# An S5 state-space layer and a SwiGLU block in one kernel: token tile 0 loaded in two halves, and the last w_down rows of two more chunks contracted in 32-row pieces

## The chip, the cores and the metric

The kernel runs on one core of one Trainium2 chip. The metric is device microseconds of that core for one execution. Its engines work in parallel and are ordered by semaphores alone: TensorE (PE; matmuls, with its weight loads shown apart as PEld), VectorE (DVE), ScalarE (ACT), GpSimd (POOL) and SyncE (SP). SyncE, ScalarE and GpSimd each have a queue from which they issue DMA transfers; "SPq" and "ACTq" in the profile are such issues. All transfers of the core run on the same 16 DMA engines.

## The reference

Input x has 2048 tokens of 512 values. They are normalized and go through two branches that are added to x:

```python
xn = _layernorm(x, axis=-1)
return x + _A_ref(xn, ...) + _B_ref(xn, B_w_gate, B_w_up, B_w_down)

def _B_ref(x, w_gate, w_up, w_down):          # F = 1376 hidden columns
    g = _silu(x @ w_gate)
    u = x @ w_up
    return (g * u) @ w_down

def _A_ref(x, ...):                           # P = 512 complex states
    Bu = jnp.einsum("bld,pd->blp", x + 0j, B_bar)
    for t in range(L):
        h = Lam_bar[None, :] * h + Bu[:, t, :]
    y = 2.0 * jnp.einsum("blp,dp->bld", hseq, Cmat).real + x * Dskip[None, None, :]
```

Inputs and output are bf16; sums are kept in f32 in PSUM.

## The kernel before

The 2048 tokens are 16 tiles of 128 (on the partitions), in 4 chunks of 4 tiles. For each chunk c there are four pieces of work on TensorE: gate and up projections (`gateup_chunk`, 10 full tiles of 128 hidden columns and a last one of 96; L446, and L501 for the last), the B projection of the state-space branch (`bproj_chunk`, L371), the down projection (`out_ffn`, L587, or in `out_pair`, L559) and the C projection of the states (`out_ssm`, L606). The two output projections of a tile add into one PSUM bank. VectorE does the layer norms, the products g*u, the rotations and the scans over time; ScalarE moves results out of PSUM (L460 with SiLU, L461, L373, L619); GpSimd issues the small copies and the stores that add onto the output, where SyncE has put x before.

The order is written out by hand, and every engine works in that order. Around it stands a small planner: `queue` puts VectorE work into a backlog with an estimated cost, `pump(us)` issues as much of it as TensorE has been given work for, `need(tag)` issues all of a kind before it is used, and `multiply` issues the products g*u that are waiting. The whole goes: a head that treats tiles 0 to 3 one by one, the rest of chunk 0's gate and up, B projections and gate/up of chunk 1, B projection of chunk 2, output of chunk 0 (`out_chunk(0)`), gate/up of chunk 2, B projection of chunk 3, output of chunk 1, gate/up of chunk 3, and the output of chunks 2 and 3 together (`out_pair`).

PSUM has 8 banks of 128x512 f32. `bank()` takes one; it comes free when its last reader is done.

The last 96 hidden columns are the concern of one part of the change. Their product g*u lies in `gu_last`, one of three buffers, with the hidden column on the partition. `product_last` forms it in place (L477). There are two ways to contract it with the last 96 rows of w_down:
- `out_last` (L594): one matmul of the full 128 partitions for each token tile, with zeros in the partitions from 96 on. Chunk 1 has it at the end of `out_ffn`; chunk 0, whose product is not ready then, in `out_end`, after the first gate/up tile of chunk 2, where its four banks are also evicted and stored (`out_leave`, L619 and L620).
- `out_rows` (L547): the 96 rows are cut into three steps of 32, and the four token tiles of a chunk are put side by side on the four groups of 32 partitions, so that four matmuls of 32 partitions each, into four banks, stand behind one another. For this `move_rows` (L186) copies the product into `gu_rows` with 12 small DMAs of GpSimd's queue, and `load_rows` (L180) loads the w_down rows four times over into the place of a B matrix that is no longer read after chunk 3's B projection. Chunks 2 and 3 have this, in `out_pair`.

In the head, SyncE's queue loads, one after the other: x tile 0 (L121), the first gate and up weights (L112), x tiles 2 and 3, the weights of hidden tile 2 (gate, then up), more weights, x tiles 4 to 7 in two transfers (L137), and the B matrices by transposing transfers (L140). ScalarE's queue loads x tile 1, whose memset (L122) makes it wait for VectorE. VectorE takes the statistics of tile 0 in one instruction (L202), those of tile 1 in two halves (L703, L705) with tile 0's normalization (L219) between them. TensorE transposes each tile (L236) and multiplies what there is with the first weights (L695); dummy matmuls (L672) fill the time before.

Of the kernel before, what the change touches and what calls it, by code (L numbers as in the profile page):

```python
# [10 lines left out]
F32 = mybir.dt.float32  # L11
BF16 = mybir.dt.bfloat16
ALU = mybir.AluOpType
ACT = mybir.ActivationFunctionType
# [9 lines left out]
def kernel(  # L24
# [17 lines left out]
    nc = tc.nc  # L42
    _, L, D = A_x.shape
# [3 lines left out]
    CW = 512  # L47
    HW = CW // 2
    NT = L // 128
    NCH = L // CW  # L50
    TPC = CW // 128
    KD = D // 128
    NQ = Pst // 128
    FT = (F + 127) // 128
# [4 lines left out]
    LA, LB = 32, 64  # L59
# [4 lines left out]
    const = ctx.enter_context(tc.tile_pool(name="const", bufs=1))  # L64
# [3 lines left out]
    opool = ctx.enter_context(tc.tile_pool(name="opool", bufs=6))  # L68
# [4 lines left out]
    def bank(shape=(128, CW), dtype=F32):  # L73
        return psum.tile(list(shape), dtype, name="ps")
# [4 lines left out]
    x_v = A_x[0].rearrange("(n p) d -> p n d", p=128)  # L79
# [5 lines left out]
    xall = const.tile([128, NT, D], BF16, name="xall")  # L85
# [10 lines left out]
    wd_sb = const.tile([128, FT, D], BF16, name="wd_sb")  # L96
# [13 lines left out]
    def load_w1(q, tiles, view, gi):  # L110
        a, b = fgroups[gi]
        q.dma_start(out=tiles[gi][:], in_=view[:, :, a * 128:min(F, b * 128)])  # L112
# [5 lines left out]
    nc.scalar.preload_act_table_set("abs_reciprocal_sqrt_and_small")  # L118


    nc.sync.dma_start(out=xall[:, 0, :], in_=x_v[:, 0, :])  # L121
    nc.vector.memset(xall[:, 1, 0:D // 2], 0.0)  # L122
    nc.scalar.dma_start(out=xall[:, 1, :], in_=x_v[:, 1, :])
    load_w1(nc.sync, wg_g, wg_v, 0)
    load_w1(nc.sync, wu_g, wu_v, 0)
# [7 lines left out]
        nc.gpsimd.dma_start(out=prm_rows[i * NQ:(i + 1) * NQ, :], in_=v.rearrange("(q j) -> q j", j=128))  # L133
    load_w1(nc.sync, wg_g, wg_v, 2)
    load_w1(nc.sync, wu_g, wu_v, 2)
    for n in (TPC, TPC + 2):
        nc.sync.dma_start(out=xall[:, n:n + 2, :], in_=x_v[:, n:n + 2, :])  # L137
    for part, src in enumerate((A_B_re, A_B_im)):
        for k in range(KD):
            nc.sync.dma_start_transpose(out=BT[:, part, k, :], in_=src[:, k * 128:(k + 1) * 128])  # L140
# [24 lines left out]

    gu_last = [const.tile([128, CW], BF16, name=f"gu_last{i}") for i in range(3)]
    for t in (*(g[LB + LA:128, :] for g in gu_last), wd_sb[LB + LA:128, FT - 1, :]):
        nc.vector.memset(t, 0.0)  # L170


    RT = 32
    part_end = const.tile([128, D // 2], F32, name="part_end")
    gu_rows = [const.tile([128, 3, 128], BF16, name=f"gu_rows{i}") for i in range(2)]
    wd_rows = BT[:, 0, 0:3, :]

    def load_rows():
        for i in range(TPC):
            nc.gpsimd.dma_start(out=wd_rows[i * RT:(i + 1) * RT], in_=B_w_down[FL:F, :].rearrange("(p f) d -> f p d", f=RT))  # L180

    def move_rows(c):

        for i in range(TPC):
            for p in range(3):
                nc.gpsimd.dma_start(out=gu_rows[c % 2][i * RT:(i + 1) * RT, p, :],  # L186
                                    in_=gu_last[c % 3][p * RT:(p + 1) * RT, i * 128:(i + 1) * 128])

    stats = const.tile([128, NT, 6], F32, name="stats")
    stats_1 = const.tile([128, 2, 6], F32, name="stats_1")  # L190
    mv = const.tile([128, NT, 2], F32, name="mv")
    ve = const.tile([128, NT], F32, name="ve")
# [8 lines left out]
    def ln_stats(n):  # L201
        nc.vector.bn_stats(out=stats[:, n, :], in_=xall[:, n, :])  # L202
        nc.vector.bn_aggr(out=mv[:, n, :], in_=stats[:, n, :])

    def rstd_act(n):

        nc.scalar.activation(out=rstd[:, n:n + 1], in_=mv[:, n, 1:2], func=ACT.Abs_reciprocal_sqrt, bias=EPS)
# [55 lines left out]
    V = nc.vector  # L263
# [205 lines left out]
    def ul(c):  # L469
        if c not in up_last:  # L470
            up_last[c] = up_p.tile([128, CW], BF16, name="ul", bufs=4)
        return up_last[c]

    def product_last(c):
        g, u = gu_last[c % 3][0:LB + LA, :], ul(c)[0:LB + LA, :]
        def mul():
            V.tensor_tensor(out=g, in0=g, in1=u, op=ALU.mult)  # L477
            if c > 1:
                move_rows(c)
        products.append(mul)  # L480

    def up_halves():

        pss = []
        for c in range(0, NCH, 2):
            ps = bank()
            pss.append(ps)
            for k in range(KD):
                for i in range(2):
                    nc.tensor.matmul(ps[i * LB:(i + 1) * LB], lhsT=wu_last[:, k, :],  # L490
                                     rhs=xnT[:, k, (c + i) * CW:(c + i + 1) * CW], start=(k == 0), stop=(k == KD - 1))
        for c in range(NCH):
            i = c % 2
            nc.scalar.copy(out=ul(c)[0:LB, :], in_=pss[c // 2][i * LB:(i + 1) * LB])
        product_last(0)
        product_last(1)

    def gateup_last(c):
        ps = bank()
        for k in range(KD):  # L500
            nc.tensor.matmul(ps[:], lhsT=w_last[:, k, :], rhs=xnT[:, k, c * CW:(c + 1) * CW],  # L501
                             start=(k == 0), stop=(k == KD - 1))
        u = ul(c)
        nc.scalar.activation(out=gu_last[c % 3][0:LB + LA, :], in_=ps[0:LB + LA], func=ACT.Silu)
        nc.scalar.copy(out=u[LB:LB + LA, :], in_=ps[LB + LA:128])
        if c > 1:
            product_last(c)

    def gateup_tile(c, fi):
        if fi == FT - 1:  # L510
            return gateup_last(c)
        psg = bank()
        gu_mm(psg, wg_g, c, fi, 0, CW)
        psu = bank()
        gu_mm(psu, wu_g, c, fi, 0, CW)
        gu_out(c, fi, psg, psu)
# [16 lines left out]
    o_tiles = {}  # L533

    def out_blocks(n):

        return ((0, D // 2), (D // 2, D - 128), (D - 128, D)) if n == NT - 1 else ((0, D),)

    def col_parts(n):
        return ((D // 2, D), (0, D // 2)) if n == NT - 1 else ((0, D),)  # L540

    def out_rows(c, step):

        for i in range(TPC):
            n, rows = c * TPC + i, slice(i * RT, (i + 1) * RT)
            lo, hi = col_parts(n)[-1]
            nc.tensor.matmul(o_tiles[n][0][:, lo:hi], lhsT=gu_rows[c % 2][rows, step, :],  # L547
                             rhs=wd_rows[rows, step, lo:hi], start=False, stop=False)

    def out_pair(c):  # L550

# [28 lines left out]
    def out_ffn(n):  # L580
        c, i = divmod(n, TPC)
        o_tiles[n] = []
        for lo, hi in out_blocks(n):
            o = bank((128, hi - lo))
            o_tiles[n].append(o)
            for fi in range(FT - 1):
                nc.tensor.matmul(o[:], lhsT=gu_tiles[c][:, fi, i * 128:(i + 1) * 128], rhs=wd_sb[:, fi, lo:hi],  # L587
                                 start=(fi == 0), stop=False)
            if c > 0:
                out_last(n, o, lo, hi, False)  # L590

    def out_last(n, o, lo, hi, stop):
        c, i = divmod(n, TPC)
        nc.tensor.matmul(o[:], lhsT=gu_last[c % 3][:, i * 128:(i + 1) * 128], rhs=wd_sb[:, FT - 1, lo:hi],  # L594
                         start=False, stop=stop)

    def out_ssm(n):
# [20 lines left out]
    def out_leave(n, o, res):  # L618
        nc.scalar.copy(out=res[:], in_=o[:])  # L619
        nc.gpsimd.dma_start(out=out_v[:, n, :], in_=res[:], accum_op=ALU.add)  # L620
# [14 lines left out]
    def step():  # L635
        for item in backlog[0:AHEAD + 1]:
            if item[2] is not None:
                item[2]()
                item[2] = None
        cost, op, _, _ = backlog.pop(0)  # L640
        op()
        owed[0] -= cost

    def pump(us):

        owed[0] += us
        while backlog and owed[0] >= backlog[0][0] * 0.5:
            step()
        if not backlog:
            owed[0] = 0.0  # L650

    def multiply(keep):

        while len(products) > keep:
            products.pop(0)()
            owed[0] -= 0.65

    def need(tag):

        while any(item[3] == tag for item in backlog):  # L660
            step()
# [8 lines left out]
    def dummy(n, cols):  # L670
        for _ in range(n):
            nc.tensor.matmul(warm[:, 0:cols], lhsT=ones[:, 0:128], rhs=ones[:, 0:cols], start=True, stop=True)  # L672
# [25 lines left out]
    allk = range(KD)  # L698
    dummy(8, CW)
    dummy(2, 128)  # L700
    ln_stats(0)
    rstd_act(0)
    nc.vector.bn_stats(out=stats_1[:, 0, :], in_=xall[:, 1, 0:D // 2])  # L703
    norm_dve(0)
# [55 lines left out]
    def gateup_chunk(c):  # L760
        for fi in [FT - 1, *range(FT - 1)]:
            gateup_tile(c, fi)
            pump(GU)
            multiply(1)
            if c == 2 and fi == 0:
                out_end(0)

    def out_chunk(c):

        multiply(0)  # L770
        for n in range(c * TPC, (c + 1) * TPC):
            out_ffn(n)
            pump(FT * 0.2163)
        if c == 0:
            need("ln3")
            up_halves()
            multiply(0)
        need(f"ssm{c}")
        need("cf")
        for n in range(c * TPC, (c + 1) * TPC):  # L780
            out_ssm(n)
            pump(2 * NQ * 0.2163)

    def out_end(c):

        for n in range(c * TPC, (c + 1) * TPC):
            o = o_tiles[n][0]
            out_last(n, o, 0, D, True)
            out_leave(n, o, opool.tile([128, D], BF16, name="res"))

    def spread(ops, others, tag, tags):

# [56 lines left out]
    queue_ssm(3)  # L849
    out_chunk(1)  # L850
    gateup_chunk(3)
    out_pair(2)

# [29 lines left out]
```

## Time and profile before

| what | us |
|---|---|
| median of 3 runs | 178.83 (178.77 to 179.09) |
| the profiled execution | 179.21 |
| its span, first to last instruction | 177.4 |
| TensorE busy | 173.1 |
| VectorE busy | 154.6 |
| ScalarE busy | 93.8 |
| GpSimd busy | 39.6 |
| DMA, mean over the span | 91 GB/s |

The granted TensorE clock is full in the whole span. The span is counted from the first instruction; the 1.8 us between it and the execution's time lie around it. Times in the chain, the timeline and the windows are us from the span's start. In the timeline a line is: start, duration, engine, line of the kernel, operation, what it writes <- what it reads, shape, count, and in brackets how long the engine had been idle and what ended that. Instructions of one kind that follow each other are merged. Matmuls overlap: one of 128x512 lasts 0.379 in the record, but the next starts 0.216 after it, so the chain, which counts from start to start, gives the cost.

### The profile page before, as it was taken

Reading aid. Unit: us, or ns where it says so; the run is one execution under the profiler, and the core shown is the slowest. Engines: PE = TensorE matmul, PEld = TensorE weight load, DVE = VectorE, ACT = ScalarE, POOL = GpSimd, SP = SyncE. Lnnn points to the kernel's source line nnn. Section 1 sums busy time; section 2 is a strip of 40 time slices with the busy share of each in tenths; the row PEclk is TensorE's granted clock in tenths of the full one; section 3 lists DMA queues with packets and bytes.
Section 4 is the critical chain, followed back from the end, with each engine's and each line's share of the span. In section 5 each row is a group of like instructions: output and inputs, shape, how many; then the busy total and the mean of one; then the engine's idle time right before and its main releaser. Section 6 shows DMA issues by size and latency. Waiting matters only on the chain.

```text
span 177.4 us, 2510 instructions
## 1 busy us (share of the span) xinstructions
PE 173.1 (98%) x922; PEld 83.1 (47%) x922; DVE 154.6 (87%) x238; ACT 93.8 (53%) x167; POOL 39.6 (22%) x61
## 2 busy tenths in 40 slices
PE   7899999999999999999999999999999999999993
PEld 2784444444444444444444444444444444464443
DVE  6879997999999996899999999999999999991033
ACT  3558898967299649924966662013866610001300
POOL 6050300000300050000709340005186330001410
PEclk9999999999999999999999999999999999999999
DMA  5999857994141015900450011005569600000652
GB/s 172 277 260 202 177 98 142 345 222 105 28 88 34 0 30 118 355 0 0 46 76 15 9 49 43 0 0 59 59 87 181 105 9 0 0 0 4 65 98 76
DMA packets 30092, 16.13 MB, mean 91 GB/s; under 512 B 19296, under 2 KB 29888, under 8 KB 30048
## 3 DMA queue, kind: packets, MB, share of 16 engines
q1 hardware_dynamic: 24800, 11.54, 28.9%
q0 software_dynamic: 4416, 3.87, 15.7%
q10 hardware_dynamic: 864, 0.56, 1.0%
q8 instruction: 7, 0.11, 0.3%
q14 instruction: 5, 0.04, 0.1%
HBM read 8.42 MB, written 5.24 MB: 77 GB/s over the span
## 4 chain that ended last, share of the span: by engine, by line
PE 94%; DMA 3%; SPq 2%; issue 0%; DVE 0%
PE ps L446 36%; PE ps L606 16%; PE ps L371 16%; PE ps L559 10%; PE ps L587 10%; DMA wu<-in_B_w_up_dram 3%; PE ps L501 2%; PE ps L695 2%; PE ps L490 1%; PE ps L594 1%; PE ps L547 1%; SPq L112 1%; SPq L126 0%; SPq L127 0%; SPq L121 0%
## 5 line engine op out<-in xcount | busy, mean ns | idle before, releaser
L446 PE MATMUL ps<-xnT,wg 128*128 128x512 bf16 x148 | 38.0, 379 | 0.0
L446 PE MATMUL ps<-xnT,wu 128*128 128x512 bf16 x148 | 38.0, 379 | 0.0
L413 DVE TENSOR_TENSOR_SCAN g<-r_t,car,u 128x512 bf16<-128x512 f32 x24 | 28.7, 1262 | 0.0
L460 ACT ACTIVATE guT<-ps 128x512 bf16<-128x512 f32 x40 | 24.4, 611 | 7.3 <-PE ps L446 5.2
L371 PE MATMUL ps<-xnT,BT 128*128 128x512 bf16 x128 | 28.3, 379 | 0.0
L606 PE MATMUL ps<-CF,wt 128*128 128x512 bf16 (+2 forms) x144 | 28.2, 355 | 0.0
L461 ACT CAST u<-ps 128x512 bf16<-128x512 f32 x40 | 23.9, 599 | 5.4 <-PE ps L446 5.3
L619 ACT CAST res<-ps 128x512 bf16<-128x512 f32 x12 | 6.8, 594 | 37.5 <-PE ps L606 37.5
L620 POOL DMA_DIRECT2D out_dram<-res x12 | 10.5, 1044 | 59.3 <-ACT res L619 59.3
L446 PEld LDWEIGHTS <-wu 128*128 128x128 bf16 x148 | 14.5, 98 | 17.5
L446 PEld LDWEIGHTS <-wg 128*128 128x128 bf16 x148 | 14.4, 98 | 17.2
L373 ACT CAST u<-ps 128x512 bf16<-128x512 f32 x32 | 18.4, 590 | 5.1 <-PE ps L371 4.9
L606 PEld LDWEIGHTS <-wt 128*128 128x128 bf16 x144 | 13.3, 98 | 14.8 <-issue 0.4
L371 PEld LDWEIGHTS <-BT 128*128 128x128 bf16 x128 | 12.5, 98 | 15.1
L587 PE MATMUL ps<-wd_sb,guT 128*128 128x512 bf16 x80 | 18.1, 379 | 0.0
L559 PE MATMUL ps<-wd_sb,guT 128*128 128x512 bf16 (+1 forms) x90 | 17.6, 355 | 0.0
L211 POOL TENSOR_TENSOR rstd<-ve,neg_half 128x4 f32<-128x4 f32 x3 | 5.2, 1728 | 47.5 <-DVE ve L210 47.5
L186 POOL DMA_DIRECT2D gu_rows<-gu_last x24 | 11.9, 505 | 9.2 <-DVE gu_last L477 6.6
L465 DVE TENSOR_TENSOR guT<-guT,u 128x1024 bf16<-128x1024 bf16 x20 | 13.5, 681 | 0.0
L559 PEld LDWEIGHTS <-guT 128*128 128x128 bf16 x90 | 8.8, 98 | 8.7
L587 PEld LDWEIGHTS <-guT 128*128 128x128 bf16 x80 | 7.8, 98 | 9.4
L611 DVE TENSOR_TENSOR res<-ps,xn_end 128x512 bf16<-128x512 f32 (+1 forms) x4 | 2.5, 626 | 10.6 <-PE ps L606 10.6
(116 smaller groups left out, 196.6 us busy)
## 6 DMA issues: line engine op xcount, KB each, us to landing
out_dram<-in_A_x_dram SPq DMA_DIRECT2D x1, 1536.0 KB, 7.0
out_dram<-res POOLq DMA_DIRECT2D x12, 128.0 KB, 3.2
out_dram<-xall POOLq DMA_DIRECT2D x3, 512.0 KB, 8.2
wd_sb<-in_B_w_down_dram SPq DMA_DIRECT2D x1, 1280.0 KB, 10.2
xall<-in_A_x_dram SPq DMA_DIRECT2D x1, 1024.0 KB, 7.0
wg<-in_B_w_gate_dram SPq DMA_DIRECT2D x1, 512.0 KB, 6.0
wu<-in_B_w_up_dram SPq DMA_DIRECT2D x1, 512.0 KB, 6.9
xall<-in_A_x_dram SPq DMA_DIRECT2D x2, 256.0 KB, 7.1
```

The lines of the kernel that those rows point to most:

```text
L186: nc.gpsimd.dma_start(out=gu_rows[c % 2][i * RT:(i + 1) * RT, p, :], in_=gu_last[c % 3][p * RT:(p + 1) * RT, i * 128:(i + 1) * 128])
L371: nc.tensor.matmul(ps[:], lhsT=BT[:, part, k, q * 128:(q + 1) * 128], rhs=xnT[:, k, c * CW:(c + 1) * CW], start=(k == 0), stop=(k == KD - 1))
L373: nc.scalar.copy(out=u_tiles[c][:, part, q, :], in_=ps[:])
L413: V.tensor_tensor_scan(out=g()[:, part, q, :], data0=r_t[:, q:q + 1].to_broadcast([128, CW]), data1=u_tiles[c][:, part, q, :], initial=ini ...
L446: nc.tensor.matmul(ps[:fs, lo:hi], lhsT=wslice(groups, fi, k), rhs=xnT[:, k, c * CW + lo:c * CW + hi], start=(k == 0), stop=(k == KD - 1))
L460: nc.scalar.activation(out=guT[:fs, fi, :], in_=psg[:fs], func=ACT.Silu)
L461: nc.scalar.copy(out=u_pair[c][:fs, fi % 2, :], in_=psu[:fs])
L465: products.append(lambda: V.tensor_tensor(out=g, in0=g, in1=u, op=ALU.mult))
L559: nc.tensor.matmul(o[:, lo:hi], lhsT=gu_tiles[k][:, fi, i * 128:(i + 1) * 128], rhs=wd_sb[:, fi, lo:hi], start=(fi == 0), stop=False)
L587: nc.tensor.matmul(o[:], lhsT=gu_tiles[c][:, fi, i * 128:(i + 1) * 128], rhs=wd_sb[:, fi, lo:hi], start=(fi == 0), stop=False)
L606: nc.tensor.matmul(o, lhsT=w_tiles[c][:, part, q, i * 128:(i + 1) * 128], rhs=CF[:, part, q, lo:hi], start=(fresh and part == 0 and q == 0 ...
L620: nc.gpsimd.dma_start(out=out_v[:, n, :], in_=res[:], accum_op=ALU.add)
```

## The change

x tile 0 is loaded as two halves of 256 columns, the first on SyncE's queue and the second on ScalarE's, ahead of tile 1, whose memset is gone. Its statistics are taken by halves too, and joined by the aggregation. x tiles 4 to 7 come in one transfer instead of two.

The last 96 hidden columns of chunks 0 and 1 are contracted by `out_rows` as well. Their product is written into the up half's buffer (`ul`) instead of onto the gate's, and `move_rows` copies it from there; `gu_last` has two buffers instead of three, `gu_rows` one for each chunk instead of two in all. `out_ffn` loses its last matmul and `out_end` is gone: chunk 0's four tiles stay in their PSUM banks until, in `out_chunk(1)` behind the down projection of chunk 1, the 24 row pieces of chunks 0 and 1 run, step by step and chunk by chunk, and chunk 0 is evicted and stored.

```diff
-    nc.sync.dma_start(out=xall[:, 0, :], in_=x_v[:, 0, :])
-    nc.vector.memset(xall[:, 1, 0:D // 2], 0.0)
+    nc.sync.dma_start(out=xall[:, 0, 0:D // 2], in_=x_v[:, 0, 0:D // 2])
+    nc.scalar.dma_start(out=xall[:, 0, D // 2:D], in_=x_v[:, 0, D // 2:D])
     nc.scalar.dma_start(out=xall[:, 1, :], in_=x_v[:, 1, :])
...
-    for n in (TPC, TPC + 2):
-        nc.sync.dma_start(out=xall[:, n:n + 2, :], in_=x_v[:, n:n + 2, :])
+    nc.sync.dma_start(out=xall[:, TPC:2 * TPC, :], in_=x_v[:, TPC:2 * TPC, :])
...
-    gu_last = [const.tile([128, CW], BF16, name=f"gu_last{i}") for i in range(3)]
+    gu_last = [const.tile([128, CW], BF16, name=f"gu_last{i}") for i in range(2)]
...
-    gu_rows = [const.tile([128, 3, 128], BF16, name=f"gu_rows{i}") for i in range(2)]
+    gu_rows = [const.tile([128, 3, 128], BF16, name=f"gu_rows{i}") for i in range(NCH)]
...
-    def move_rows(c):
+    def move_rows(c, product):
...
-                nc.gpsimd.dma_start(out=gu_rows[c % 2][i * RT:(i + 1) * RT, p, :],
-                                    in_=gu_last[c % 3][p * RT:(p + 1) * RT, i * 128:(i + 1) * 128])
+                nc.gpsimd.dma_start(out=gu_rows[c][i * RT:(i + 1) * RT, p, :],
+                                    in_=product[p * RT:(p + 1) * RT, i * 128:(i + 1) * 128])
...
-        g, u = gu_last[c % 3][0:LB + LA, :], ul(c)[0:LB + LA, :]
+        g, u = gu_last[c % 2][0:LB + LA, :], ul(c)[0:LB + LA, :]
         def mul():
-            V.tensor_tensor(out=g, in0=g, in1=u, op=ALU.mult)
-            if c > 1:
-                move_rows(c)
+            to = g if c == NCH - 1 else u
+            V.tensor_tensor(out=to, in0=g, in1=u, op=ALU.mult)
+            move_rows(c, to)
...
-            if c > 0:
-                out_last(n, o, lo, hi, False)
...
-    ln_stats(0)
+    for h in range(2):
+        nc.vector.bn_stats(out=stats_0[:, h, :], in_=xall[:, 0, h * (D // 2):(h + 1) * (D // 2)])
+    nc.vector.bn_aggr(out=mv[:, 0, :], in_=stats_0[:])
...
             multiply(1)
-            if c == 2 and fi == 0:
-                out_end(0)
...
     def out_chunk(c):
...
+        if c == 1:
+            for step in range(3):
+                for k in range(2):
+                    out_rows(k, step)
+            for n in range(TPC):
+                out_leave(n, o_tiles[n][0], opool.tile([128, D], BF16, name="res"))
         need(f"ssm{c}")
         need("cf")
```

More of the change, by code (lines that the diff above doesn't have):

```diff
@@ L180, in load_rows @@
             nc.gpsimd.dma_start(out=wd_rows[i * RT:(i + 1) * RT], in_=B_w_down[FL:F, :].rearrange("(p f) d -> f p d", f=RT))
-    def move_rows(c):
+    def move_rows(c, product):
         for i in range(TPC):
             for p in range(3):
-                nc.gpsimd.dma_start(out=gu_rows[c % 2][i * RT:(i + 1) * RT, p, :],
-                                    in_=gu_last[c % 3][p * RT:(p + 1) * RT, i * 128:(i + 1) * 128])
+                nc.gpsimd.dma_start(out=gu_rows[c][i * RT:(i + 1) * RT, p, :],
+                                    in_=product[p * RT:(p + 1) * RT, i * 128:(i + 1) * 128])
     stats = const.tile([128, NT, 6], F32, name="stats")
+    stats_0 = const.tile([128, 2, 6], F32, name="stats_0")
     stats_1 = const.tile([128, 2, 6], F32, name="stats_1")
@@ L503, in gateup_last @@
         u = ul(c)
-        nc.scalar.activation(out=gu_last[c % 3][0:LB + LA, :], in_=ps[0:LB + LA], func=ACT.Silu)
+        nc.scalar.activation(out=gu_last[c % 2][0:LB + LA, :], in_=ps[0:LB + LA], func=ACT.Silu)
         nc.scalar.copy(out=u[LB:LB + LA, :], in_=ps[LB + LA:128])
@@ L546, in out_rows @@
             lo, hi = col_parts(n)[-1]
-            nc.tensor.matmul(o_tiles[n][0][:, lo:hi], lhsT=gu_rows[c % 2][rows, step, :],
-                             rhs=wd_rows[rows, step, lo:hi], start=False, stop=False)
+            nc.tensor.matmul(o_tiles[n][0][:, lo:hi], lhsT=gu_rows[c][rows, step, :],
+                             rhs=wd_rows[rows, step, lo:hi], start=False, stop=(c == 0 and step == 2))
     def out_pair(c):
@@ L588, in out_ffn @@
                                  start=(fi == 0), stop=False)
-            if c > 0:
-                out_last(n, o, lo, hi, False)
     def out_last(n, o, lo, hi, stop):
         c, i = divmod(n, TPC)
-        nc.tensor.matmul(o[:], lhsT=gu_last[c % 3][:, i * 128:(i + 1) * 128], rhs=wd_sb[:, FT - 1, lo:hi],
+        nc.tensor.matmul(o[:], lhsT=gu_last[c % 2][:, i * 128:(i + 1) * 128], rhs=wd_sb[:, FT - 1, lo:hi],
                          start=False, stop=stop)
@@ L782, in out_chunk @@
             pump(2 * NQ * 0.2163)
[L784 to L789, printed above, removed]
     def spread(ops, others, tag, tags):
```

## The prediction

> **What bounds the kernel now.** I read the page's engine line first, then the chain of waits in order of time, then the timeline around the two places that the change touches, and last the DMA engines' load in half-microsecond stretches.
>
> ```profile
> PE 173.1 (98%) x922; PEld 83.1 (47%) x922; DVE 154.6 (87%) x238; ACT 93.8 (53%) x167; POOL 39.6 (22%) x61
> ```
>
> TensorE is busy for nearly the whole span. The chain says from where on it alone counts:
>
> ```profile
> 3.71 4.94 DMA wu<-in_B_w_up_dram
> 8.65 0.05 issue
> 8.70 1.28 PE ps L695 x16
> ...
> 84.09 0.86 PE ps L594 x4
> ...
> 109.56 0.22 PE ps L594
> ...
> 159.34 1.40 PE ps L547 x18
> 160.74 13.97 PE ps L606 x80
> ```
>
> From 8.70 us to the output additions everything is TensorE, without a gap. So the time is (when the third up-projection weight tile lands) + (TensorE work behind it) + (the output tail). L594 is the work that the change takes out of chunks 0 and 1, L547 what it puts in. The start, by the timeline:
>
> ```profile
> 0.74 0.40 SPq L121 DMA_DIRECT2D xall<-in_A_x_dram  x1
> 1.07 0.40 ACTq L123 DMA_DIRECT2D xall<-in_A_x_dram  x1
> 2.91 0.69 DVE L202 BATCH_NORM_STATS2 stats<-xall 128x6 f32<-128x512 bf16 x1 [0.59 <-DMA xall<-in_A_x_dram]
> 3.73 0.39 DVE L703 BATCH_NORM_STATS2 stats<-xall 128x6 f32<-128x256 bf16 x1
> 8.13 0.22 PE L266 MATMUL ps<-ident,prm_rows 128*128 128x128 bf16 x1
> 8.70 0.61 PE L695 MATMUL ps<-xnT,wu 128*128 128x256 bf16 x4 [0.34 <-DMA wu<-in_B_w_up_dram]
> ```
>
> Tile 0 sets when TensorE begins (4.56), but TensorE, ready again some 0.06 after 8.13, then waits for weights until 8.70. The row pieces as chunks 2 and 3 already use them, in TensorE's timeline:
>
> ```profile
> 158.08 1.25 PE L559 MATMUL ps<-wd_sb,guT 128*128 128x256 bf16 x10
> 159.27 1.47 PE L547 MATMUL ps<-BT,gu_rows 32*128 32x512 bf16 x24
> 160.67 0.61 PE L606 MATMUL ps<-CF,wt 128*128 128x512 bf16 x2
> ```
>
> and the DMA engines (last two columns: share of 16 engines, GB/s):
>
> ```profile
> 1.50:2.00 0.50, 0.50 (x2) 0.15 (x1) 0.50 (x2) 0.50 (x1) 0.50 (x1) 1.00 0.27 86
> 2.00:2.50 0.50, 0.50 (x3) 0.21 (x2) 0.31 (x2) 0.02 (x1) 0.50 (x2) 1.00 0.86 297
> 2.50:3.00 0.50, 0.50 (x3) 0.23 (x2) 0.09 (x1) 0.00 (x0) 0.50 (x2) 1.00 0.88 235
> 4.00:4.50 0.50, 0.21 (x3) 0.03 (x1) 0.50 (x3) 0.05 (x1) 0.30 (x1) 1.00 1.11 329
> ```
>
> They are full from 3 us on (1.03 to 1.16 of them in most stretches up to 6.5, as transfers overlap), not before.
>
> **The row pieces.** Removed: 8 full matmuls of 0.216 each (0.86 for four in the chain), 1.73. Added: 24 pieces in 6 rounds of four. The same 24 run from 159.27 to 160.67, 1.40; in front, ten matmuls of 0.109 from 158.08 should have been followed at 159.17, so the entry costs 0.10 more. Sum 1.50, saving 0.23. (Three of those 24 are half as wide; each shares its round with full ones, so I add nothing.) Ends: 0.33 if the entry gap is not the pieces' doing, and 0.13 if a second such gap comes at the exit that the 1.40 does not hold.
> The trace thus shows a gap on going over to 32-row pieces. The Trainium skill, TensorEngine Tiling (Array Packing), Key Properties, says that changing the tiling mode drains TensorE, which speaks against this edit; its table's 4x for contractions up to 32 would make 24 pieces cost 6 x 0.216 = 1.30, an estimate, and the saving 0.43. By this trace the drain holds, so 0.23.
>
> **What the pieces need.** GpSimd issues 24 more moves, 0.5 each (12 took 5.94 at 93.39): some 12 us from 82.5. It is free then, since the chunk 0 stores of 85.5 go behind. The chunk 2 moves slip from 93.4 to some 94.5, needed at 159; the reload of the last w_down rows still waits for TensorE (104.03, some 0.9 earlier now), lands 2.3 after its last issue at 106.2, so by 108.5, and is first read near 115. Cover 6 us; without it TensorE would wait by the excess.
> Chunk 0 keeps four PSUM banks until then, which leaves four for chunk 2's gate/up and chunk 3's B projections. A bank comes round after three other groups of 0.86, 2.59; ScalarE starts an eviction as the group ends (0.28 idle before each) and takes 0.60. Cover 1.9. Chunk 2's gate now overwrites gu_last of chunk 0, so ScalarE's SiLU at 82.40 waits for that product, first of two in 82.06 to 82.81: 0.1 late, inside the same cover. The four copies of 2.06 move from 84.6 to some 117, where ScalarE is idle (0.59 busy between 107.4 and 117.0); their stores are 4 x 0.9 on GpSimd, done before the skip stores at 128.6. VectorE's order stays; scans took 9.50 beside GpSimd's stores and 9.51 without, so I charge nothing for more GpSimd traffic. TensorE runs 0.86 ahead of before in chunk 2: the fifth pair's cast (98.8) reuses a buffer that VectorE frees at 97.1, cover 1.7 down to 0.85.
>
> **Tile 0 in halves.** VectorE's 0.69 becomes 0.39 + 0.42 (L703, L705), of which the first can run before the second half is there. First half: issued at 0.74, lands 1.8 (64 KB, ScalarE's queue, at the end of the kernel) to 2.1 later, 2.55 to 2.9. Second: the memset it no longer waits for ended at 1.04, so issue at 0.78 to 1.07, landing 2.6 to 3.2. The aggregation, 3.64 now, starts between 3.36 and 3.72: from 0.28 earlier to 0.08 later. I take 0.25 earlier, as ScalarE's queue has nothing ahead of this load. Tile 1 goes out one issue later (0.46 on SyncE), 1.24 to 1.53, and lands 2.1 on, 3.3 to 3.6, about when VectorE comes to it. Tile 2 (issue 2.21 + 3.4 = 5.6) keeps its statistics at 5.68 and its normalization until 7.48; its transposes, 7.91 now, may move to 7.66. So TensorE is ready for the late weights at 7.94 instead of 8.19.
> That is worth nothing while those weights land at 8.65. But the profiled execution took 179.21 (177.4 of span and 1.81 around it), 0.38 over the median of 178.83, and this is TensorE's only long wait behind the start: I put the 0.38 there, and the median's matmuls at 8.32. SyncE's queue now holds 64 KB less ahead of these weights, 0.21 at about 300 GB/s; ScalarE's queue moves them before 3 us, when the engines had room. So 8.32 becomes 8.11, later than 7.94: gain 0.21. Ends: 0 (weights unmoved) and 0.38 (weights no longer in the way).
>
> **The rest.** Tiles 4 to 7 as one load instead of two (issues 5.36 and 5.9, the later landed 7.3 on, 13.2): first read at 14.48, cover 1.3. SyncE is free for the weight transposes up to 0.9 sooner, first needed at 19.1. Two memsets fewer (0.17 and some 0.27) lie in VectorE's wait for tile 0. Nothing.
>
> **Sum.** 178.83 - 0.23 - 0.21 = 178.39; in the profiled execution's own terms 179.21 - 0.23 = 178.98 were its weights as late again.
>
> **Rivals.**
> Weights hold (178.60): the landing at 8.3 to 8.65 does not move and covers tile 0 whole; only 0.23 comes. For it: 4.94 from issue to landing against 3.3 for the gate tile just ahead, a delay that 64 KB need not touch. The other cause with the same end: both halves land together at 2.9 and 0.81 of statistics takes the place of 0.69. The Trainium skill, DMA: Bandwidth & Descriptors, gives a DMA a fixed cost of about 2.0 us whatever its size; the 64 KB and 128 KB stores on ScalarE's queue (1.8 and 1.7) agree.
> Tile 1 late (slower): it stands behind tile 0's second half, and VectorE, in order, reads it ahead of normalizing tile 0. SyncE's x loads took 3.4; so would it: 1.53 + 3.4 = 4.93 against 3.73, TensorE ready at 9.4 instead of 8.32, 1.1 lost, 179.7. The delay must first eat the 0.13 between 8.19 and 8.32 and then the 0.23 of the pieces, so it decides from a landing near 4.1; 0.36 later still and the kernel is measurably slower. Against it: 2.1 on this queue before.
> Pieces stall (178.9): a PSUM bank or the reload comes late by 0.5, which is more than both gains. Against it: the covers above.
>
> **How the numbers follow.** Both gains 0.58 (0.05 of it under 0.36 together, since the second may be anything from 0 to 0.38), weights hold 0.27, tile 1 late 0.12, stall or no saving 0.03. The first case is the likeliest because the engines' idle share before 3 us is there to be used; the second follows because no row shows how the late landing came about. About 0.2%, 0.36 us, is what a measurement here tells from no change: faster 0.53, same 0.35, slower 0.12. The range runs from 178.1 (0.33 and 0.38 gained) to 178.95 (the late tile at a third of its price, 0.35, less the 0.23 of the pieces).
>
> **What would show it.** After: no L594 in chunks 0 and 1; 24 more L547 pieces near 115, 1.5 from one full matmul's slot to the next; no TensorE wait between 8.7 and the tail; first half's statistics before 2.9 and the aggregation near 3.4; the third up tile's matmuls near 8.1 to 8.5. Wrong if TensorE waits on PSUM or GpSimd's moves in 84 to 117, if tile 1 lands after 4.1, or if the weights land later than 8.65.

## The result and the profile after

The changed kernel takes 181.08 us, median of 5 executions (179.44 to 181.30); the kernel before takes 178.86 (178.77 to 179.09). The ratio is 1.0104, 95% interval 1.0087 to 1.0121: it is slower by 1%. The profiled execution of the changed kernel took 181.08, its span 179.3.

The loss lies in the first 14 us, and behind them the changed kernel is the faster one. This is the chain of waits of the changed kernel in order of time (start, duration, what; line numbers have moved by up to two, so L693 is the former L695, L604 the former L606):

```profile
1.20 3.80 DMA xall<-in_A_x_dram
5.00 0.02 issue
5.02 0.43 DVE stats L703
5.45 0.33 DVE xall L219
5.78 0.05 issue
5.82 0.60 PE ps L236 x4
...
7.71 0.43 PE ps L236 x4
8.13 2.50 PE ps L693 x28
10.64 0.22 PE ps L236 x4
...
14.26 6.91 PE ps L446 x32
...
108.59 8.63 PE ps L587 x40
117.22 1.41 PE ps L547 x24
118.63 7.01 PE ps L604 x32
...
162.57 13.97 PE ps L604 x80
```

The first line is the load of tile 1, which before was nowhere on the chain. The last matmul ends at 176.54, as it ended at 174.71 before. From the first full-width matmuls on (14.26 here, 12.21 before) that is 162.28 against 162.50: the body gained 0.22. The head lost 14.26 - 12.21 = 2.05. In the row pieces' place the chain shows 1.41 for 24 of them, and 8.63 for the 40 matmuls ahead, without a full last contraction in between.

How tile 1 holds up tile 0, in the timeline of the changed kernel (start, duration, engine, line; the brackets hold the idle time before and what ended it):

```profile
0.77 0.40 ACTq L122 DMA_DIRECT2D xall<-in_A_x_dram  x1
1.20 0.46 ACTq L123 DMA_DIRECT2D xall<-in_A_x_dram  x1
1.20 0.42 SPq L112 DMA_DIRECT2D wg<-in_B_w_gate_dram  x1
2.92 0.75 DVE L700 BATCH_NORM_STATS2 stats<-xall 128x6 f32<-128x256 bf16 x2 [1.02 <-DMA xall<-in_A_x_dram]
3.71 0.21 DVE L701 BATCH_NORM_AGGREGATE mv<-stats 128x2 f32<-128x12 f32 x1
5.02 0.43 DVE L703 BATCH_NORM_STATS2 stats<-xall 128x6 f32<-128x256 bf16 x1 [1.10 <-DMA xall<-in_A_x_dram]
5.37 0.40 DVE L219 TENSOR_SCALAR xall<-xall,mv,rstd 128x512 bf16<-128x512 bf16 x1
5.82 0.60 PE L236 MATMUL ps<-ident,xall 128*128 128x128 bf16 x4 [1.25 <-DVE xall L219]
```

Tile 0's mean and variance are there at 3.92 and ScalarE's reciprocal root soon after. VectorE's next instruction in order, however, is the first half of tile 1's statistics, and tile 1 lands at 5.00. Tile 0 is normalized only behind that, and TensorE stands idle for 1.25 us.

What happens then is a second loss. The chain above has four transposes in 0.43 at 7.71 and four others of the same shape in 0.22 at 10.64: matmuls of 128 columns follow each other at 0.107 us up to about 9.5, and at 0.056 from there on. The profile's clock column shows the full clock throughout. From the first transposes to the first full-width matmul the changed kernel takes 14.26 - 5.82 = 8.44.

### The profile page after: what moved, and what is told of

Same layout as the page of the kernel before. It is cut to its first block, busy times and chain, and to the rows that moved or that the text cites. A ratio compares the mean times of both kernels' runs of the same rounds, so it can differ in the third digit from the quotient of the medians.

```text
span 179.3 us, 2570 instructions
## 1 busy us (share of the span) xinstructions
PE 174.5 (97%) x938; PEld 84.5 (47%) x938; DVE 154.4 (86%) x237; ACT 94.2 (53%) x167; POOL 51.3 (29%) x85
## 4 chain that ended last, share of the span: by engine, by line
PE 95%; DMA 2%; DVE 1%; ACT 0%; issue 0%
PE ps L446 36%; PE ps L604 16%; PE ps L371 15%; PE ps L559 10%; PE ps L587 10%; PE ps L693 4%; DMA xall<-in_A_x_dram 2%; PE ps L501 2%; PE ps L547 2%; PE ps L490 1%; PE ps L236 1%; DVE stats L703 0%; ACT L118 0%; PE ps L670 0%; DVE xall L219 0%; DVE res L609 0%
## 5 line engine op out<-in xcount | busy, mean ns | idle before, releaser
L446 PE MATMUL ps<-xnT,wg 128*128 128x512 bf16 x148 | 38.0, 379 | 0.0
L446 PE MATMUL ps<-xnT,wu 128*128 128x512 bf16 x148 | 38.0, 379 | 0.0
L604 PE MATMUL ps<-CF,wt 128*128 128x512 bf16 (+2 forms) x144 | 28.2, 356 | 0.0
L185 POOL DMA_DIRECT2D gu_rows<-ul x36 | 17.6, 498 | 18.1 <-DVE ul L478 18.1
L446 PEld LDWEIGHTS <-wu 128*128 128x128 bf16 x148 | 14.5, 98 | 17.4
L446 PEld LDWEIGHTS <-wg 128*128 128x128 bf16 x148 | 14.5, 98 | 17.2
L604 PEld LDWEIGHTS <-wt 128*128 128x128 bf16 x144 | 13.3, 98 | 15.0 <-issue 0.8
L587 PE MATMUL ps<-wd_sb,guT 128*128 128x512 bf16 x80 | 17.6, 379 | 0.0
```

The costliest lines, as they stand in the source:

```text
L185: nc.gpsimd.dma_start(out=gu_rows[c][i * RT:(i + 1) * RT, p, :], in_=product[p * RT:(p + 1) * RT, i * 128:(i + 1) * 128])
L446: nc.tensor.matmul(ps[:fs, lo:hi], lhsT=wslice(groups, fi, k), rhs=xnT[:, k, c * CW + lo:c * CW + hi], start=(k == 0), stop=(k == KD - 1))
L604: nc.tensor.matmul(o, lhsT=w_tiles[c][:, part, q, i * 128:(i + 1) * 128], rhs=CF[:, part, q, lo:hi], start=(fresh and part == 0 and q == 0 ...
```

## The experiments

**The body alone**: the changed kernel with the head of before.

```diff
-    nc.sync.dma_start(out=xall[:, 0, 0:D // 2], in_=x_v[:, 0, 0:D // 2])
-    nc.scalar.dma_start(out=xall[:, 0, D // 2:D], in_=x_v[:, 0, D // 2:D])
+    nc.sync.dma_start(out=xall[:, 0, :], in_=x_v[:, 0, :])
+    nc.vector.memset(xall[:, 1, 0:D // 2], 0.0)
...
-    for h in range(2):
-        nc.vector.bn_stats(out=stats_0[:, h, :], in_=xall[:, 0, h * (D // 2):(h + 1) * (D // 2)])
-    nc.vector.bn_aggr(out=mv[:, 0, :], in_=stats_0[:])
+    ln_stats(0)
```

and tiles 4 to 7 in two loads.

> The row pieces alone: the head is that of before (tile 0 whole, the memset ahead of tile 1, tiles 4 to 7 in two loads), everything behind it that of the changed kernel. Theory 'the head lost it': the two traces give 162.51 us from the first full-width matmuls to the last one before (12.21 to 174.72) and 162.29 after (14.26 to 176.55), so 0.22 less: 178.65, between 178.5 and 178.8. Rival 'the row pieces cost part of it' (more GpSimd work, four PSUM banks held for 35 us): 179.0 or more.

Measured: 178.56 (178.48 to 178.86), beside 178.96 for the kernel before on the same chip; ratio 0.9982, 0.9973 to 0.9990. This version beats both kernels. Its chain, from the first full-width matmuls to the end (one line number further on, L447 for L446):

```profile
12.07 6.91 PE ps L447 x32
...
115.03 1.41 PE ps L548 x24
...
160.38 13.97 PE ps L605 x80
```

174.35 - 12.07 = 162.28, the same body as in the changed kernel. So the row pieces gain 0.22 by the traces, and the timed interval, 0.18 to 0.48, holds that.

**The head alone**: tile 0 in halves, no memset, one load for tiles 4 to 7, in the body of before. The edit is the first two hunks of the change, on the loads, and the statistics of tile 0; `gu_last` keeps its three buffers.

> The head alone: tile 0 in halves, no memset, tiles 4 to 7 in one load, and the body of before. Theory 'the head lost it': 181.08 + 0.22 = 181.3, between 179.5 and 181.6 as the changed kernel itself varies from 179.4 to 181.3, with tile 1 landing near 5.0. Rival: 179.0 or less.

Measured: 180.48, ratio 1.0086, 1.0055 to 1.0117. The head alone loses what the changed kernel lost. Its eight executions lie in two groups: 179.45, 179.53, 179.85, 179.97, and 180.99, 181.07, 181.43, 181.52. The profiled one (179.85) is of the first group, and its chain tells the two losses apart:

```profile
1.19 3.67 DMA xall<-in_A_x_dram
4.86 0.02 issue
4.88 0.43 DVE stats L705
...
7.13 0.22 PE ps L236 x4
...
12.82 6.91 PE ps L446 x32
```

and TensorE's timeline of the same run has the idle gap:

```profile
5.68 0.40 PE L236 MATMUL ps<-ident,xall 128*128 128x128 bf16 x4 [1.11 <-DVE xall L219]
```

Tile 1 is as late and TensorE idles nearly as long, but the matmuls go at full pace at once (0.22 for four). From 5.68 to 12.82 that is 7.14, against 8.44 in the changed kernel's profile: half pace costs 1.30 in that profile. The means of the two groups, 179.70 and 181.25, are 1.55 apart, so this is most of what divides them; the changed kernel's own executions (179.44, and four from 180.75 to 181.30) divide the same way.

**Tile 1 ahead of the weights**, halves kept.

```diff
-    nc.scalar.dma_start(out=xall[:, 1, :], in_=x_v[:, 1, :])
+    nc.sync.dma_start(out=xall[:, 1, :], in_=x_v[:, 1, :])
```

> The changed kernel with one thing moved: tile 1 is loaded by SyncE's queue, behind the first half of tile 0 and ahead of the first weights; the second half stays on ScalarE's queue. Theory 'race': tile 1 came late since its load left at the same time as the first weights (1.20) and shared the engines with them; ahead of them it lands by 3.6, tile 0's transposes start at 4.6 and the time is 178.4 to 178.9. Rival 'halves': the half rows of 512 bytes on two queues slow all transfers between 2.4 and 3.2 (99 GB/s between 2.5 and 3.0 where the kernel before had 235); then tile 1 or the first weights land after 4.2 here too, and the time is over 179.5.

Measured: 178.93 (178.72 to 179.67), ratio 1.0006, 0.9994 to 1.0019: the loss is gone, as "race" expects, though 0.03 over its range. The load leaves at the same 1.20 as in the changed kernel, ahead of the weights instead of beside them, and VectorE reads it at 3.83. The timeline:

```profile
1.20 0.42 SPq L123 DMA_DIRECT2D xall<-in_A_x_dram  x1
2.91 0.75 DVE L700 BATCH_NORM_STATS2 stats<-xall 128x6 f32<-128x256 bf16 x2 [1.01 <-DMA xall<-in_A_x_dram]
3.70 0.21 DVE L701 BATCH_NORM_AGGREGATE mv<-stats 128x2 f32<-128x12 f32 x1
3.83 0.37 DVE L703 BATCH_NORM_STATS2 stats<-xall 128x6 f32<-128x256 bf16 x1
4.65 0.40 PE L236 MATMUL ps<-ident,xall 128*128 128x128 bf16 x4
```

It also shows what the halves are worth with the race out of the way. Their statistics start at 2.91, as those of the whole tile did, and take 0.75 instead of 0.69; the aggregation starts at 3.70 instead of 3.64. The loads show why: the first half of 64 KB landed 2.1 us after its issue and the second 2.3, where the whole tile of 128 KB had taken 2.1. Halving the transfer did not shorten it. Against the body alone this version is 0.37 slower in the medians; its tile 2, one load further back, landed at 2.69 + 3.7 = 6.4, and VectorE waits 0.55 for it.

**Tile 1 late, tile 0 whole**: the kernel before, with tile 1's load held back past the first weights.

```diff
-    nc.vector.memset(xall[:, 1, 0:D // 2], 0.0)
+    for _ in range(2):
+        nc.vector.memset(xall[:, 1, :], 0.0)
```

> The kernel before with two full memsets of tile 1 in place of one half memset, so that tile 1's load leaves at some 1.45 instead of 1.07, behind the first weights (1.20) and not ahead of them; tile 0 stays whole. Theory 'race': tile 1 lands near 5, VectorE waits for it ahead of normalizing tile 0, 180.5 to 181.5. Rival 'halves': tile 1 lands 0.4 later, at 3.6, before VectorE comes to it at 3.73, and the time stays at 178.9.

Measured: 180.87 (179.63 to 181.66), ratio 1.0096, 1.0063 to 1.0130. The loss of the changed kernel comes back with no half loads at all, in the same two groups (three executions from 179.63 to 179.80, four from 180.87 to 181.66). The chain:

```profile
1.60 3.24 DMA xall<-in_A_x_dram
4.84 0.02 issue
4.87 0.43 DVE stats L704
```

The load left at 1.60, later than meant, and landed at 4.84. Issued at 1.07, ahead of the first weights at 1.20, the same load had taken 2.1. The Trainium skill, DMA: Bandwidth & Descriptors, Queues, rings and completion order, says that each DMA engine serves the queues in turn, a packet at a time. The traces agree as far as they go: in the changed kernel tile 1 and the first gate weights leave together at 1.20 and land together, 3.8 later each.

**Tile 0 normalized first**, in the changed kernel.

```diff
-    nc.vector.bn_stats(out=stats_1[:, 0, :], in_=xall[:, 1, 0:D // 2])
     norm_dve(0)
+    nc.vector.bn_stats(out=stats_1[:, 0, :], in_=xall[:, 1, 0:D // 2])
```

> The changed kernel with VectorE's normalization of tile 0 put ahead of the first half statistics of tile 1, so that tile 0 no longer waits behind tile 1's load (which stays late, near 5.0). Theory 'in-order wait': tile 0's transposes start near 4.5 instead of 5.82, TensorE's gap of 1.25 goes, and with it the executions of 181; but tile 1 is still late and its chain then sets the time: 179.0 to 179.7. Rival 'tile 0's wait is the whole of it': 178.4 to 178.7. Rival 'the wait in VectorE's order plays no part': 180.5 or more.

Measured: 179.21 (179.02 to 179.52), ratio 1.0020, 1.0011 to 1.0029. Two instructions exchanged on VectorE take 1.9 off the median, though the load is late as before (4.70). The timeline:

```profile
4.20 0.41 DVE L219 TENSOR_SCALAR xall<-xall,mv,rstd 128x512 bf16<-128x512 bf16 x1 [0.27 <-ACT rstd L207]
4.67 0.40 PE L236 MATMUL ps<-ident,xall 128*128 128x128 bf16 x4 [0.20 <-DVE xall L219]
4.72 0.43 DVE L704 BATCH_NORM_STATS2 stats<-xall 128x6 f32<-128x256 bf16 x1
5.92 0.72 PE L693 MATMUL ps<-xnT,wg 128*128 128x128 bf16 x8 [0.62 <-DVE xnT L243]
```

The transposes are back at 4.67 and at full pace. A part of the wait has moved: tile 0's copy out of PSUM now stands behind tile 1's statistics, and its matmuls begin at 5.92.

**More dummy matmuls**, in the changed kernel, so that TensorE is not idle while tile 1 is late.

```diff
     dummy(8, CW)
-    dummy(2, 128)
+    dummy(14, 128)
```

> The changed kernel with 14 instead of 2 small dummy matmuls behind the 8 large ones, so that TensorE is busy until 5.2 to 5.7 instead of 4.6; tile 1 is as late as in the changed kernel. Theory 'cold matmuls': of the 2.05 that the changed kernel loses in the head, some 1.3 is the late tile and the rest is TensorE's matmuls at half pace (0.107 from start to start instead of 0.056) until 9.6, which begin so after the idle gap in some executions and not in others; without the gap the pace is full in all, no execution is over 180.3, and the median is 179.3 to 179.9. Rival 'the half pace has another cause': executions of 181 go on, median over 180.3.

Measured: 179.66, ratio 1.0040, 1.0027 to 1.0053, and no execution over 179.78. TensorE in this run:

```profile
0.78 5.07 PE L670 MATMUL ps<-const-bfloat16-1.0 128*128 128x512 bf16 x22 [0.78 <-PEq L864]
5.64 0.63 PE L236 MATMUL ps<-ident,xall 128*128 128x128 bf16 x4
6.07 0.63 PE L670 MATMUL ps<-const-bfloat16-1.0 128*128 128x128 bf16 x4
...
7.00 0.39 PE L236 MATMUL ps<-ident,xall 128*128 128x128 bf16 x4
```

Twelve matmuls of no use take 1.42 off the median (1.13 off the mean) and do away with the upper group. The first transposes and the four dummies behind them are still slow here (0.63 for four, against 0.60 in the changed kernel), though TensorE has not been idle since 0.78; the next ones at 7.00 are not. The lateness of tile 1 is untouched; what went is the half pace from 7 to 9.5.

**The wait for the third up weights**: the body alone, with the four matmuls that wait for them put behind six that do not.

```diff
     params_a(pp)
-    head_mm(1, 0, 2, allk, (2,))
     norm_dve(3)
     head_mm(0, 2, 3, range(0, HK), range(H))
+    head_mm(1, 0, 2, allk, (2,))
```

> The row pieces alone (178.56), with the four matmuls that wait for the up weights of hidden tile 2 put behind six matmuls of tile 2 that do not need them. If the executions of the median wait for those weights, as the prediction had it, TensorE goes on at 8.5 instead of 8.55 to 8.70 and has six matmuls done by then: 0.1 to 0.3 less, 178.3 to 178.45. If they do not wait: 178.5 to 178.6.

Measured: 178.96 (178.87 to 179.27), ratio 1.0007, 0.9999 to 1.0016, where the body alone had 0.9982 in another set of runs. Neither reading expected that: it is slower. TensorE now waits for VectorE's copies of tile 2 instead, so that one wait stands in the place of another:

```profile
8.67 0.49 PE L694 MATMUL ps<-xnT,wg 128*128 128x128 bf16 x6 [0.21 <-DVE xnT L244]
```

In this execution there was no wait for the weights to avoid: they landed 4.0 after their issue at 3.71. So the run does not tell what such a wait costs.

**Tiles 4 to 7 in one load**, in the body alone.

```diff
-    for n in (TPC, TPC + 2):
-        nc.sync.dma_start(out=xall[:, n:n + 2, :], in_=x_v[:, n:n + 2, :])
+    nc.sync.dma_start(out=xall[:, TPC:2 * TPC, :], in_=x_v[:, TPC:2 * TPC, :])
```

> The row pieces alone, with tiles 4 to 7 in one load as in the changed kernel, and the head else that of before. The tiles are first read at 14.48 and landed by 13.2: no change, 178.5 to 178.65. Were the one load a part of the loss: 179 or more.

Measured: 178.63 (178.58 to 179.12), ratio 0.9990, 0.9981 to 0.9999. The one load is no part of the loss. Its profiled execution (178.68) shows TensorE at the place where the kernel before waited:

```profile
8.22 0.22 PE L266 MATMUL ps<-ident,prm_rows 128*128 128x128 bf16 x1
8.28 0.60 PE L693 MATMUL ps<-xnT,wu 128*128 128x256 bf16 x4
```

There is no wait: the weights, issued at 3.71, had landed 3.9 later.

## Why the prediction was wrong, and where it was right

The forecast was 178.39 and counted on 0.21 gained in the head; the head lost 2.05.

**The step that failed** is the one on tile 1: "lands 2.1 on, 3.3 to 3.6, about when VectorE comes to it". It landed 3.80 after its issue, at 5.00. The issue time was nearly right (1.20, against 1.24 to 1.53). The duration was carried over from a load that left before the first weights, to one that leaves beside them. In the kernel before, the memset ended in time to let the load go at 1.07, after tile 0 and still ahead of the weights at 1.20; in the changed kernel it goes at 1.20, behind the half of tile 0 that ScalarE's queue issues from 0.77 on. The prediction had this as its rival "Tile 1 late", with the right place and the right mechanism of the loss, VectorE waiting in its order, and gave it 0.12. That its landing of 4.93 came so near to 5.00 is luck: it is 1.53 + 3.4, where the run has 1.20 + 3.80. It put the lateness on the half load ahead in the queue, and the run with tile 0 whole shows tile 1 nearly as late (4.84) with no half load there.

**A term missing from that rival** is TensorE's pace. It priced the late tile at 1.1. The start of TensorE was 1.26 later (5.82 against 4.56); then came 1.30 for half pace, less the wait for weights at 8.70 that the kernel before had in its profile and the changed one no longer meets. That wait follows from the other three, 1.26 + 1.30 - 2.05 = 0.51, and the timeline before agrees (8.70 against 8.19 for readiness). The gap did not bring the half pace on. TensorE has it from its first dummy matmul in every trace here; the weight loads of the large dummies, one for each, are some 0.43 us apart, where matmuls of 512 columns later follow each other at 0.216. In the changed kernel:

```profile
3.73 0.15 PEld L670 LDWEIGHTS <-const-bfloat16-1.0 128*128 128x128 bf16 x1 [0.28 <-issue]
4.15 0.15 PEld L670 LDWEIGHTS <-const-bfloat16-1.0 128*128 128x128 bf16 x1 [0.28 <-issue]
```

What differs is when it ends: near 3.7 in the kernel before (whose ten dummies last 3.42, against 3.78 in the changed kernel), between 4.3 and 4.6 in the body alone, near 6.6 with more dummies, where there was no gap at all. In the changed kernel's profile it had not ended when the gap began, and lasted to 9.5; in the head alone it ended within the gap, so that the matmuls behind it are fast. By these traces the gap put the end of the half pace off, and the more-dummies run, which fills the gap and has no slow execution, shows that this hangs on TensorE's activity. The Trainium skill, TensorE: Matmul & The Clock Gate, Part 1, says that TensorE's clock is halved until it has been busy for a window of about 3.4 us, and that the window runs freely, so that the same kernel differs from run to run. The traces agree in the pace (0.107 and 0.056) and in the two groups; no run shows the length of the window (where no gap of 1 us or more came first, full pace began 2.9 to 5.8 us after the first dummy). That the window's phase sorts executions into the groups is argued from that section of the Trainium skill and not shown by a run.

**Tile 0 "0.25 earlier"**: it came 0.07 later (3.71 against 3.64). The end of the range that was passed over, both halves landing together near 2.9, is about what happened, here and with tile 1 out of the way. What the prediction cited from the Trainium skill, DMA: Bandwidth & Descriptors, a fixed cost of about 2.0 us whatever the size, which that page states for transfers that GpSimd issues, agrees with the landings of 2.1 to 2.3, on SyncE's and ScalarE's queues.

**The weights "at 8.32" in the median execution, 8.11 after**: not borne out. This is the load of the third up weights, issued at 3.71 in both kernels, with its time to landing in the kernel before and in the changed one:

```profile
wu<-in_B_w_up_dram SPq DMA_DIRECT2D x1, 128.0 KB, 4.9
wu<-in_B_w_up_dram SPq DMA_DIRECT2D x1, 128.0 KB, 4.0
```

It is that late in two traces of the ten, the kernel before (8.65) and the body alone (8.51). In the other eight it landed between 7.5 and 7.8, before TensorE was ready, and in none near 8.3. Among the eight are runs that load these weights in the same order on the same queue as the kernel before, so the late landing belongs to the execution and not to the kernel. To put the 0.38 between the profiled execution and the median down to this wait may have been right: the profiled execution of the body alone has the wait too (its matmuls go on at 8.55) and took 178.86, 0.30 over its median, and that with one load for tiles 4 to 7 has none and took 178.68, 0.05 over its own. But an execution without the wait had nothing to gain there. How often the kernel before has it, and what makes the load late, stays open.

**The row pieces**: 0.23 predicted, 0.22 found in the traces of two kernels. The cost was read right from chunks 2 and 3, as TensorE's timeline of the changed kernel shows:

```profile
114.69 2.54 PE L587 MATMUL ps<-wd_sb,guT 128*128 128x512 bf16 x11
117.16 1.47 PE L547 MATMUL ps<-BT,gu_rows 32*128 32x512 bf16 x24
118.56 1.68 PE L604 MATMUL ps<-CF,wt 128*128 128x512 bf16 x7
```

Eleven matmuls of 0.216 from 114.69 would be followed at 117.06; the first piece starts 0.10 behind that, and the next full matmul 1.40 after it: 1.50 again. What stood as covered was covered. GpSimd issued its 36 moves of chunks 0 to 2 in one stretch and was done with the reload in time, and in the whole trace TensorE waits only at the start:

```profile
PE ps L236 <- DVE xall L219: 1.3, 1, 1.3
PE ps L670 <- PEq L864: 0.8, 1, 0.8
```

These are all of TensorE's waits in the changed kernel. One load for tiles 4 to 7 costing nothing was right too.

## What to carry to other kernels

A load's duration belongs to its place in the traffic: before moving an issue by a tenth of a microsecond, look at which other transfer it then leaves beside, and who stands in line behind its reader. What stands in front of a load on its queue sets when it leaves: tile 1 went at 1.07 behind a half memset, at 1.60 behind two full ones and at 1.20 behind another load. When a change to the start and a change to the body come together, try them apart: here the body's gain was hidden under a loss nine times its size.

## What the runs showed of the hardware that was not expected

A load of 128 KB took 2.1 to 2.3 us when issued 0.13 to 0.46 ahead of 256 KB of weights, and 3.2 to 3.8 when issued beside or behind them. Transfers of 64 KB and of 128 KB at the empty start took the same 2.1 to 2.3. TensorE began at half pace in every trace and went over to full pace at different times, 3.7 to 6.6 us into the span where it was not idle for 1 us or more before. An idle gap of 1.25 put this off to 9.5 in the changed kernel's profile, which cost 1.30, while a profiled execution of the head alone with a gap of 1.11 did not pay it; the profile's clock column stayed at full in both.
